# Attention and a gated MLP on one core: the low part of v's last tokens moves to GpSimd, the table is called early, and the written-out order is replaced

## The chip, the cores and the metric

The kernel runs on one core of a Trainium2 chip. Five instruction streams run side by side there: TensorE (matmuls; its weight loads are a row of their own in the profile, PEld), VectorE (DVE), ScalarE (ACT), GpSimd (POOL) and SyncE (SP), which issues the DMAs here. Each stream runs its instructions in the order in which they were written; semaphores make one wait for another. The metric is device time in microseconds, less is better.

## The reference

Causal attention over 4 batches, 12 heads, 448 tokens and 64 channels a head is followed by a gated MLP over all tokens of a batch, everything in float32:

```python
scores = scale * np.matmul(q, k.transpose(0, 1, 3, 2))
scores = np.where(mask, -1000000000.0, scores)
attn = np.exp(scores - np.max(scores, axis=-1, keepdims=True))
attn = attn / (np.sum(attn, axis=-1, keepdims=True) + 1e-09)
x = np.matmul(attn, v)              # heads side by side: (4, 448, 768)
h = x @ w_in                        # (4, 448, 1024), then gelu (tanh form)
u, v = h[..., :512], h[..., 512:]
v_n = (v - mu) / np.sqrt(var + 1e-06) * g_ln
v_s = np.einsum('ts,bsd->btd', w_sg, v_n) + b_sg[None, :, None]
out = x + (u * v_s) @ w_out
```

## The kernel before

Heads go in pairs: 24 pairs, six for each batch. For a pair, TensorE makes the scores (line 431, two groups of matmuls), DVE adds the mask and finds the maximum of each row (446), and ACT takes exponentials with the row sums (454, ten for a pair of five widths). The probabilities are then transposed: for the first eight pairs by TensorE (496), with the results copied out of PSUM by ACT or DVE (503, 501), for the others by DVE (484) and four DMAs. TensorE multiplies them with the values (522), DVE scales the result by the reciprocal row sums (549), and the product x is kept in a rounded high part and the low part that is left over (555 to 560).

The MLP of a batch has four kinds of matmul groups, all on line 577. Group v makes the half of h that is normed, for four blocks of tokens (128, 128, 128 and 64); group u makes the other half; group s multiplies the normed v with w_sg; group o multiplies with w_out. Precision is kept by splitting each operand into a high and a low part, each in the rounded format that TensorE reads fast, and adding three products. The weights are split when they arrive (366 to 374 for w_in and w_out, 350 to 353 for w_sg): ACT and DVE take the words apart, GpSimd rounds and subtracts.

For the first three token blocks of v, ACT writes the high part (630) and GpSimd subtracts it from the value (631). The last block has 64 tokens. Its high part goes to partitions 0 to 63 of the tile `vn3` (635) and its low part to partitions 64 to 127 of the same tile, so that one matmul takes both. Before the change, DVE makes that low part (636). The matmuls of group s that read `vn3` come last in each of its four groups.

Nothing of the order is left to a scheduler. Every step is recorded with its engine and an estimated duration (`od.add`, and `act`, `dve`, `pool_tt`, `pe`, `dma` over it), and a list of 1883 numbers, `ORDER`, says in which sequence the steps are written. The sequence on one engine is the sequence of that engine's steps in the list. PSUM has eight banks that all tiles there share: a new tile takes the bank that was given up first, and its first writer waits for the last reader of the old one. The estimated durations and the flag `port` were for the search that made the list; they don't reach the chip.

Before the first use of an exponential, ACT must load its table. Step 3 of the list, an exponential of one column into a spare tile, is meant to call for that load:

```python
    od.add("act", 0.2, lambda: nc.scalar.activation(out=pad[:, 0:1], in_=mhalf, func=AF.Exp), ["sm0"], ["table"])
```

Nothing depended on it, and in the old list it stands in the middle. Seven matmuls on a zeroed tile (339) are for warming TensorE up; their place is also the list's.

Of the kernel before, what the change touches and what calls it, by code (L numbers as in the profile page):

```python
# [12 lines left out]
AF = mybir.ActivationFunctionType  # L13
# [212 lines left out]
def attention_gated_mlp(ctx: ExitStack, tc: tile.TileContext, qk, vP, w_in, g_ln, w_sgT, b_sg, w_out, out):  # L226
# [100 lines left out]
    od.add("dve", 0.75, consts2, w=["P0", "sm0"])  # L327
    od.add("pool", 2.4, consts3, w=["P", "sm", ("wsg", "pad")])

    od.add("act", 0.2, lambda: nc.scalar.activation(out=pad[:, 0:1], in_=mhalf, func=AF.Exp), ["sm0"], ["table"])  # L330

    def warm():
        w = wz.t.bitcast(BF16)
# [432 lines left out]
```

## Time and profile before

| | us |
|---|---|
| median of 3 runs | 339.13 (338.38 to 340.37) |
| profiled execution | 337.29 |
| its span | 335.5 |
| busy in the span: TensorE, DVE, ACT, GpSimd | 324.1, 251.0, 208.5, 175.9 |
| mean granted clock of TensorE, as a share of full speed | 0.994 |

The span runs from the first to the last instruction of the program; the profiled execution has 1.8 us around it. Busy time of TensorE is the time in which some matmul was under way, so it also holds the small gaps between pipelined matmuls. An engine's share of the whole span is a mean over stages with different limits: ACT, for instance, is busy all the time early and little later.

### The profile page before, as it was taken

What the parts mean: (1) busy time and instruction counts of PE and PEld (TensorE: products, weight loads), DVE (VectorE), ACT (ScalarE), POOL (GpSimd) and SP (SyncE); (2) the same over time, 40 slices, a digit from 0 to 9 for tenths busy, and PEclk for the clock granted to TensorE, in tenths of its full rate; (3) what the DMA queues carried; (4) which work ended last, traced back from release to release, by engine and by line L of the source; (5) the groups of instructions that cost most, each with busy time, mean ns of one, the idle gap of its engine ahead of it and who ended that gap; (6) DMA issues with size and microseconds to landing.
All of it is one profiled execution on the core that took longest, in us unless ns stands there. A gap on an engine that the chain in (4) does not pass through costs nothing.

```text
span 335.5 us, 7568 instructions
## 1 busy us (share of the span) xinstructions
PE 324.1 (97%) x2590; PEld 266.3 (79%) x2591; DVE 251.0 (75%) x762; ACT 208.5 (62%) x674; POOL 175.9 (52%) x225
## 2 busy tenths in 40 slices
PE   5699999999999999999999999999999999999995
PEld 3467678768887987878888978878989987889994
DVE  4899898999999888967977597889788531644613
ACT  1999999999894637666784526486674302355210
POOL 4258766888986964020535942014256824132691
PEclk9899999999999999999999999999999999999999
DMA  7889968595583688638747858739437440010004
GB/s 227 312 247 307 277 218 267 177 288 160 130 265 103 178 215 235 197 98 226 217 127 214 229 150 204 195 95 243 101 104 206 91 159 3 0 55 2 18 36 164
DMA packets 30965, 56.55 MB, mean 169 GB/s; under 512 B 6096, under 2 KB 15056, under 8 KB 30928
## 3 DMA queue, kind: packets, MB, share of 16 engines
q1 hardware_dynamic: 30928, 56.08, 57.5%
q8 instruction: 20, 0.33, 0.4%
q14 instruction: 17, 0.14, 0.1%
HBM read 33.39 MB, written 5.90 MB: 117 GB/s over the span
## 4 chain that ended last, share of the span: by engine, by line
PE 93%; ACT 4%; DMA 1%; DVE 1%; issue 0%; ACTq 0%; DVEq 0%
PE m L577 65%; PE o L522 13%; PE s L431 11%; ACT P L454 3%; PE ty L496 2%; PE tx L496 2%; DMA qk<-in_qk_dram 1%; PE m L339 0%; ACT L454 0%; ACT vn L366 0%; ACT B L503 0%; DVE s L446 0%; DVE res L702 0%; DVE ngm L446 0%; ACTq L454 0%
## 5 line engine op out<-in xcount | busy, mean ns | idle before, releaser
L454 ACT ACTIVATE P<-s,ngm 128x320 f32<-128x320 f32 (+3 forms) x240 | 102.7, 460 | 28.1 <-DVE ngm L446 19.7
L446 DVE CUSTOM_DVE_ANT_0 s<-s,mask 64x64 f32<-64x64 f32 (+3 forms) x192 | 77.6, 435 | 7.5 <-PE s L431 5.8
L577 PE MATMUL m<-win,x 128*128 128x512 f32 (+1 forms) x264 | 65.9, 399 | 0.0
L577 PE MATMUL m<-g,wout 128*128 128x448 f32 x288 | 61.1, 367 | 0.0
L577 PE MATMUL m<-x,win 128*128 128x448 f32 x288 | 61.1, 367 | 0.0
L577 PEld LDWEIGHTS m<-x,win 128*128 128x128 f32 x288 | 53.9, 188 | 5.0
L577 PEld LDWEIGHTS m<-g,wout 128*128 128x128 f32 x288 | 53.9, 188 | 5.0
L577 PEld LDWEIGHTS m<-win,x 128*128 128x128 f32 (+1 forms) x264 | 47.4, 183 | 11.7
L454 ACT ACTIVATION_READ_ACCUMULATOR P<-s,ngm 128x1 f32 (+1 forms) x240 | 55.1, 233 | 0.0
L431 PE MATMUL s<-qk 64*64 64x64 f32 (+5 forms) x768 | 45.2, 371 | 5.0 <-DMA qk<-in_qk_dram 4.4
L431 PEld LDWEIGHTS s<-qk 64*64 64x64 f32 x768 | 30.7, 139 | 21.6 <-issue 8.5
L522 PE MATMUL o<-B,vraw 128*64 128x64 f32 (+4 forms) x672 | 45.0, 291 | 0.0
L522 PEld LDWEIGHTS o<-B,vraw 128*64 128x64 f32 x672 | 32.8, 137 | 12.7 <-issue 4.5
L484 DVE STREAM_TRANSPOSE P<-P 128x1024 f32<-128x1024 f32 x32 | 38.2, 1224 | 0.7 <-DMA B<-P 0.6
L577 PE MATMUL m<-wsg,vn 128*128 128x448 f32 x176 | 38.3, 369 | 0.0
L621 POOL TENSOR_TENSOR mv<-mv,mhalf 128x1 f32<-128x1 f32 (+1 forms) x16 | 10.0, 626 | 49.0 <-DVE mv L619 40.7
L577 PEld LDWEIGHTS m<-wsg,vn 128*128 128x128 f32 x176 | 32.6, 188 | 3.6 <-DVE vn L636 0.4
L558 POOL TENSOR_TENSOR x<-xt,x 128x448 fp32r<-128x448 f32 x24 | 27.5, 1148 | 14.5 <-ACT x L557 14.2
L702 DVE TENSOR_TENSOR res<-m,res 128x448 f32<-128x448 f32 (+1 forms) x25 | 14.8, 603 | 23.2 <-PE m L577 15.2
L586 DVE SCALAR_TENSOR_TENSOR tmp<-tmp,m 128x448 f32<-128x448 f32 (+1 forms) x28 | 17.9, 640 | 16.2 <-ACT tmp L585 16.0
L673 POOL TENSOR_TENSOR tmp<-tmp,g 128x448 f32<-128x448 f32 x16 | 18.3, 1152 | 18.8 <-DVE tmp L669 18.8
L585 ACT ACTIVATE tmp<-m 128x448 f32<-128x448 f32 (+1 forms) x28 | 15.5, 562 | 20.3 <-PE m L577 19.2
(76 smaller groups left out, 410.8 us busy)
## 6 DMA issues: line engine op xcount, KB each, us to landing
B<-P SPq DMA_DIRECT2D x64, 256.0 KB
qk<-in_qk_dram SPq DMA_DIRECT2D x24, 448.0 KB
vn<-in_w_in_dram SPq DMA_DIRECT2D x12, 512.0 KB
vraw<-in_vP_dram SPq DMA_DIRECT2D x24, 256.0 KB
rb<-rd SPq DMA_DIRECT2D x24, 224.0 KB
out_dram<-res SPq DMA_DIRECT2D x9, 448.0 KB
g<-in_w_out_dram SPq DMA_DIRECT2D x16, 192.0 KB
out_dram<-res SPq DMA_DIRECT2D x5, 224.0 KB
```

What stands on the lines that cost most here:

```text
L431: nc.tensor.matmul(out=s[z][bk].t[64 * h:64 * h + 64, col:col + n], lhsT=qk_.t[r, 0, q0:q0 + 64], rhs=qk_.t[r, 1, k0:k0 + n], start=True, ...
L446: nc.vector.tensor_tensor_reduce(out=o, in0=i, in1=mk, scale=-0.125, scalar=3e38, op0=ALU.add, op1=ALU.min, accum_out=ngm[ib[z]][c][0:m])
L454: act(n, lambda c=c, m=m, k0=k0, n=n, bk=bk, col=col, off=off, kc=kc, i=i, z=z: nc.scalar.activation(out=P[i][0:m, off:off + n], in_=s[z][ ...
L484: dve(PW, lambda z=z: nc.vector.transpose(A[ia][:, :, :, z, :].rearrange("p g t k -> p t g k"), P[ib[z]]), Pk[z] + [kp], Ak, 1.105)
L496: nc.tensor.transpose(out, P[ib[z]][:, col:col + 128], ident)
L522: nc.tensor.matmul(out=dst(o.t[r]), lhsT=vr.t[:, c, r], rhs=src(z), start=first and n == 0, stop=last and n == len(lst) - 1)
L558: pool_tt(S, lambda: nc.gpsimd.tensor_tensor(out=y.t[:, S + 64:], in0=x.t, in1=f(y.t)[:, 0:S], op=ALU.subtract), [x, y], [(y, 1)])
L577: nc.tensor.matmul(out=ps.t[0:l().shape[1], 0:n], lhsT=l(), rhs=rr(), start=(k == 0), stop=(k == len(mms) - 1))
L585: act(n, lambda: nc.scalar.activation(out=z(), in_=h(), func=AF.Square), [ps], [t])
L586: dve(n, lambda: nc.vector.scalar_tensor_tensor(out=z(), in0=z(), scalar=1.0 / GC, in1=h(), op0=ALU.add, op1=ALU.mult), [ps], [t])
L673: pool_tt(S, lambda z=z, u=u: nc.gpsimd.tensor_tensor(out=z(), in0=z(), in1=u.t, op=ALU.mult), [u], [t])
L702: dve(hi - lo, lambda rr=rr, ps=ps, z=z, lo=lo, hi=hi: nc.vector.tensor_tensor(out=rr.t[:, z, lo:hi], in0=ps.t[:, lo:hi], in1=rr.t[:, z, l ...
```

## The change

Three things change in the program, and with them the list.

1. The low part of v's last 64 tokens: DVE's subtraction goes. ACT writes the high part a second time, to partitions 64 to 127 of `vn3`, and copies the value to partitions 64 to 127 of its own tile; GpSimd then subtracts in place, with everything on those partitions. A batch has one DVE step less and two ACT steps and one GpSimd step more.
2. Every exponential of the attention depends on step 3, the call for the table.
3. The list has 1891 numbers, from a search in which DVE and GpSimd exclude each other where both need the SBUF port that they share. It differs from its beginning on. Step 3 stands early, for instance, GpSimd's two blocks of constants (steps 0 and 2) trade places, and so do two of DVE's memset blocks (1 and 4); some of w_out's loads and splits (steps 12 to 83 are those of w_in, later numbers those of w_out) come earlier and w_in's later.

Some estimates of durations and two `port` flags change too; they were for the search alone.

```diff
-    84, 85, 86, 1, 4, 0, 2, 89, 87, 90, 96, 88, 95, 98, 91, 92, 97, 99, 93, 94, 125, 126, 128, 127, 12, 18, 13, 103,
-    101, 116, 166, 332, 14, 129, 130, 20, 15, 102, 100, 134, 131, 135, 136, 19, 104, 138, 110, 111, 24, 344, 350, 356,
...
+    2, 4, 84, 85, 1, 0, 125, 86, 126, 127, 89, 87, 3, 90, 96, 88, 95, 98, 97, 91, 92, 99, 344, 345, 350, 93, 94, 101,
+    100, 128, 346, 129, 103, 108, 110, 104, 136, 102, 132, 133, 12, 18, 166, 109, 138, 111, 140, 13, 142, 20, 134,
...
-    od.add("act", 0.2, lambda: nc.scalar.activation(out=pad[:, 0:1], in_=mhalf, func=AF.Exp), ["sm0"], ["table"])
+    od.add("act", 1.35, lambda: nc.scalar.activation(out=pad[:, 0:1], in_=mhalf, func=AF.Exp), ["sm0"], ["table"])
...
-                    [s[z][bk], ("ngm", i, c), kp, ks] + ([("P", i, k - 1)] if k == 1 else [("P", i, 2)] if k == 4 else []),
+                    [s[z][bk], ("ngm", i, c), kp, ks, "table"] + ([("P", i, k - 1)] if k == 1 else [("P", i, 2)] if k == 4 else []),
...
-        od.add("dve", 0.42, inv, sk + [ks], [("rT", ip)])
+        od.add("dve", 0.573, inv, sk + [ks], [("rT", ip)])
...
-            tensor=rd[ip].tensor, offset=rd[ip].offset, ap=[[512, 8], [0, 16], [1, S]])), [("rd", ip)], [rb], 320e3, dur=0.56)
+            tensor=rd[ip].tensor, offset=rd[ip].offset, ap=[[512, 8], [0, 16], [1, S]])), [("rd", ip)], [rb], 360e3, dur=0.56)
...
-                t, z = gelu2(hs, m, DH)
+                t, z = gelu2(hs, m, DH, port=True)
...
-                out=z(), in_=z(), func=AF.Identity, scale=mv.t[0:m, 1:2], bias=mv.t[0:m, 2:3]), [mv], [t], True)
+                out=z(), in_=z(), func=AF.Identity, scale=mv.t[0:m, 1:2], bias=mv.t[0:m, 2:3]), [mv], [t], True, 2)
...
-                dve(DH, lambda y=y, z=z: nc.vector.tensor_tensor(out=y.t[64:128], in0=z(), in1=f(y.t)[0:64],
-                                                                 op=ALU.subtract), [t, y], [(y, 1)])
+                act(DH, lambda y=y, z=z: nc.scalar.activation(out=y.t[64:128], in_=z(), func=AF.Copy), [t], [(y, 1)], True)
+                act(DH, lambda t=t, z=z: nc.scalar.activation(out=t.t[64:128], in_=z(), func=AF.Copy), [], [t], True)
+                pool_tt(DH, lambda y=y, t=t: nc.gpsimd.tensor_tensor(out=y.t[64:128], in0=t.t[64:128],
+                                                                     in1=f(y.t)[64:128], op=ALU.subtract), [t], [(y, 1)])
```

## Rows read from the trace of the kernel before

**Rows 1.** The chain of waits in order of time: start us, us, what.

```profile
3.92 1.88 PE s L431 x8
...
8.37 1.40 ACT P L454 x5
...
13.46 0.56 ACT vn L366
...
18.85 0.61 ACT P L454 x2
...
20.00 0.66 PE ty L496 x4
...
276.38 55.46 PE m L577 x263
...
331.87 0.62 DVE res L702
```

**Rows 2.** Busy time by stretches: stretch, length, busy of each engine, granted clock, DMA.

```profile
20.00:40.00 20.00, 19.95 (x226) 13.94 (x228) 18.91 (x79) 20.00 (x79) 14.24 (x17) 1.00 0.91 271
60.00:80.00 20.00, 20.00 (x186) 14.54 (x185) 19.65 (x68) 19.32 (x67) 16.39 (x22) 1.00 0.78 238
80.00:100.00 20.00, 20.00 (x121) 17.36 (x120) 18.96 (x63) 17.45 (x54) 18.25 (x24) 1.00 0.59 168
100.00:120.00 20.00, 20.00 (x170) 16.90 (x172) 17.73 (x44) 11.17 (x37) 16.64 (x21) 1.00 0.55 147
```

**Rows 3.** Timeline of DVE and ACT in the front: start, us, engine, instruction, idle before.

```profile
5.94 0.23 DVE L446 CUSTOM_DVE_ANT_0 s<-s,mask 64x64 f32<-64x64 f32 x1 [3.88 <-PE s L431]
...
7.07 1.28 ACT L454 ACT_TABLE_LOAD   x1 [7.07 <-DVE ngm L446]
...
21.18 0.40 ACT L454 ACTIVATE P<-s,ngm 64x64 f32<-64x64 f32 x1
...
21.47 0.69 ACT L503 ACTIVATE B<-tx 128x512 f32<-128x512 f32 x1
21.95 0.62 ACT L454 ACTIVATE P<-s,ngm 128x320 f32<-128x320 f32 x1
...
22.45 0.79 ACT L366 ACTIVATE vn<-vn 128x512 f32<-128x512 f32 x1
```

**Rows 4.** Timeline of TensorE, 20 to 24 us.

```profile
20.97 1.67 PE L339 MATMUL m<-tmp 128*128 128x512 bf16 x6
22.58 1.64 PE L431 MATMUL s<-qk 64*64 64x448 f32 x26
```

**Rows 5.** Waits of the weight loads, 22 to 332 us: total, times, longest.

```profile
PEld s L431 <- ACT B L503: 0.8, 2, 0.4
...
PEld m L577 <- DVE vn L636: 0.4, 2, 0.2
```

**Rows 6.** Groups by form: busy us, mean ns of one, idle before.

```profile
L631 POOL TENSOR_TENSOR vn<-tmp,vn 128x512 fp32r<-128x512 f32 x12 | 15.9, 1331 | 18.5 <-ACT vn L630 18.4
...
L635 ACT ACTIVATE vn<-tmp 64x512 fp32r<-64x512 f32 x4 | 2.5, 630 | 0.1
```

**Rows 7.** The view of line 636: durations are min/median/max in ns.

```profile
L636 DVE TENSOR_TENSOR vn<-tmp,vn x4: 685/685/2120, 97.8 to 308.4; 64x512 fp32r<-64x512 f32 x4
```

**Rows 8.** Timeline around the low part's subtraction, batches 0 and 2.

```profile
98.51 0.30 PEld L577 LDWEIGHTS m<-wsg,vn 128*128 128x128 f32 x2 [0.18 <-DVE vn L636]
...
243.78 2.27 POOL L689 TENSOR_TENSOR res<-x 128x448 f32<-128x448 f32 x2
...
244.48 2.12 DVE L636 TENSOR_TENSOR vn<-tmp,vn 64x512 fp32r<-64x512 f32 x1 [1.02 <-ACT vn L635]
...
246.65 0.30 PEld L577 LDWEIGHTS m<-wsg,vn 128*128 128x128 f32 x2 [0.25 <-DVE vn L636]
```

**Rows 9.** Busy time and granted clock of TensorE, 14 to 18 us.

```profile
14.00:18.00 4.00, 3.64 (x28) 0.57 0.51 157
```

More of the change, by code (lines that the diff above doesn't have):

```diff
@@ L579, in group, with gelu2 @@
             pe(per * len(mms[a:a + cut]), go, rd, [ps])
-    def gelu2(ps, m, n, dst=None):
+    def gelu2(ps, m, n, dst=None, port=False):
         t = buf(three, "tmp", [128, 512])
@@ L586, in gelu2 @@
         dve(n, lambda: nc.vector.scalar_tensor_tensor(out=z(), in0=z(), scalar=1.0 / GC, in1=h(), op0=ALU.add,
-                                                      op1=ALU.mult), [ps], [t])
+                                                      op1=ALU.mult), [ps], [t], port=port)
         act(n, lambda: nc.scalar.activation(out=z(), in_=z(), func=AF.Tanh, scale=GS * GC), [], [t], True)
@@ L590, in gelu2 @@
         dve(n, lambda: nc.vector.scalar_tensor_tensor(out=z() if dst is None else d.t, in0=z(), scalar=1.0, in1=h(),
-                                                      op0=ALU.add, op1=ALU.mult), [ps, t], [d])
+                                                      op0=ALU.add, op1=ALU.mult), [ps, t], [d], port=port)
         return t, z
@@ L622, in mlp @@
                 out=mv.t[0:m, 1:2], in0=mv.t[0:m, 1:2], in1=mhalf[0:m], op=ALU.pow), ["sm0"], [mv])
-            od.add("dve", 0.07, lambda mv=mv, m=m: nc.vector.tensor_scalar(
+            od.add("dve", 0.125, lambda mv=mv, m=m: nc.vector.tensor_scalar(
                 out=mv.t[0:m, 2:3], in0=mv.t[0:m, 0:1], scalar1=mv.t[0:m, 1:2], scalar2=-1.0, op0=ALU.mult, op1=ALU.mult),
```

177 rows, old and new, of the table ORDER are left out of this document.

## Prediction

> **What bounds the kernel now.** The profiled execution took 337.29 us, 335.5 of them its span; the runs shown have the median 339.13 (338.38 to 340.37). I make the sum against the profiled one and carry the difference over to the median.
>
> I read the chain of waits in order of time first. The reader is to see three stretches in it. From 3.92 to 8.37 it runs through the scores of the first pair, their maxima on DVE and the load of the activation table on ACT. From 8.37 to 20.0 it stays on ACT, but for fractions of a microsecond. From 20.0 to 331.8 it is TensorE alone, and then comes one DVE addition and the store [rows 1, 3]. So whatever TensorE does first at full density comes sooner or later, and the end moves with it, unless another engine then makes TensorE wait.
>
> The busy time by stretches says who could. Between 20 and 40 us ACT is busy for 20.00 of 20 us and DVE for 18.91; between 60 and 80 us DVE for 19.65 and ACT for 19.32; between 80 and 100 us GpSimd has its peak, 18.25. After 100 us ACT falls to 11.17 [rows 2]. So up to some 80 us three engines run nearly full beside TensorE, and later TensorE alone decides.
>
> Third, the waits of TensorE's weight loads from 22 us on: those on ACT are fractions of a microsecond (on ACT's evictions 0.8 in two), and those on the low part of v's last tokens, DVE's instruction that the change takes away, are 0.4 in two [rows 5]. TensorE runs just behind ACT, and there is little to win after 22 us.
>
> **The change, part by part.**
>
> *The table.* The first ACT instruction of the old list is an exponential. The load of the table stands before it: ACT sits idle for 7.07 us, then loads for 1.28, and the first exponential starts at 8.37 [rows 3, 1]. The new list puts the small exponential that calls for the table first on ACT and makes every other exponential depend on it. It needs only DVE's memsets, and DVE is done with those 3.88 us before its first maximum at 5.94 [rows 3]. So the load is over by about 3.6 us, in time in which ACT has nothing to do; that idle time is its cover, and without it the 1.30 (8.37 less 7.07) would come back. This takes 1.30 us off the chain.
>
> The Trainium skill, in ScalarE: Activation LUTs, What ACT_TABLE_LOAD costs, gives 1283 ns for the load and about 1380 more for a drain. The load agrees with the row; the drain isn't there, since the next ACT instruction starts 0.02 us after the load, and by the page's 2.66 us the sum would be 1.36 us lower.
>
> *The order in the front.* The scores of pair 3 are the first work of TensorE's dense stretch whose place both lists share: they start at 22.58, after warm-up matmuls that end there [rows 4]. In the new list their second bank waits for the same eviction as before, the one of pair 1 that starts at 21.47 [rows 3] and ends near 22.2. Both lists have 31 ACT steps up to it. The old has two exponentials of pair 2 (448 and 64 wide) and a third split of w_in that the new has not; the new has one exponential of 320 and one split of w_out instead, beside the small one for the table. From start to start a 448-wide one, a split, a 64-wide and a 320-wide one cost 0.61 (the piece at 18.85) and 0.56 (at 13.46) [rows 1], 0.29 (21.18 to 21.47) and 0.50 (21.95 to 22.45) [rows 3]; I price the narrower w_out split at the same 0.56. That is 0.61 + 0.29 - 0.50 = 0.40 less, and 1.30 from the table: 1.7. So the eviction ends near 20.5, and the scores, whose start no longer trails the warm-up matmuls (the new list mixes these among the transposes), start there: 2.1 us earlier than 22.58.
>
> *What ACT lets TensorE keep.* The rest of ACT's work isn't gone, only listed later. For each matmul that waits for an ACT step I added the ACT work listed ahead of that step and the TensorE work listed behind the matmul, both at the durations of the trace. The largest sum bounds the end. In the old list it is 43.1 + 275.5 us (100 ACT steps ahead of the first scores of pair 8, 2103 matmuls behind); in the new one 56.7 + 261.6 us (134 and 1996, at the second scores of pair 9). A step of ACT costs 0.3 to 0.6 as above, a matmul of the late groups 55.46/263 = 0.21 [rows 1]. The sums differ by 0.3, the start of ACT by 1.30: the end may come 1.6 us earlier by this bound, 0.5 less than the front gives. I take 1.6.
>
> DVE's bound I can't fix so well. Its first maximum waits for scores [rows 3] that don't move, so it gains nothing at the start, and it is 91 to 98% busy up to 100 us [rows 2]. If it is the engine that TensorE trails, the gain is between 0 and 1.6.
>
> *The low part of v's last 64 tokens.* Out go four subtractions on DVE, 685 ns in the median and 2120 once [rows 7]; in come eight copies on ACT like the one that was there (630 ns) and four subtractions on GpSimd, for which the nearest row is the one over 128 partitions, 1331 ns [rows 6]. All lie behind 80 us, where ACT has room, so the engines' time costs nothing; what it would cost without that room is 5.0 us of ACT. The path from a batch's last v group to the first matmul that reads its low part grows by two copies and by 1331 against 685: 1.26 + 0.65 = 1.9 us. In batches 0 and 2, at 98.5 and 246.65, TensorE's weights waited for just this subtraction [rows 5, 8], so there is no slack in the old list; the new one puts 21.0 instead of 19.2 us of TensorE work between the two in batch 0, and 19.9 instead of 16.4 in batch 2. That leaves -0.1 and +1.6. In batches 1 and 3 nothing waited; the lists leave the same work in batch 1 and 0.6 more in batch 3. So I take nothing for it, with 0 to 1.9 us a batch as its bounds.
>
> *The port.* The trace shows what the shorthand means: DVE's subtraction with both inputs in SBUF starts at 244.48 beside GpSimd's additions (243.78 to 246.05) and takes 2.12 us; TensorE's weights wait for it until 246.65 [rows 8]. An order that avoids such meetings can win on TensorE's path the 0.4 of [rows 5] at most; I take 0.2. The other estimates that the diff changes (the Identity's, the transfer's, the reciprocal's) are numbers for the planner and alter no instruction; they act by the list alone.
>
> *The end.* Both lists finish with one 448-wide addition and its store, as in the row at 331.87 [rows 1]: nothing.
>
> Sum: -1.6 - 0.2 = -1.8 us. The profiled execution would take 335.5 (a span of 333.7) and the median 339.13 - 1.8 = 337.3.
>
> **The rivals.**
>
> *DVE hands it back.* TensorE starts its dense stretch 2.1 us earlier and then trails DVE, whose start hasn't moved. For it: DVE's 19.65 of 20 us; against it: TensorE's weights wait longer for ACT's evictions than for DVE's subtraction [rows 2, 5]. Half the gain is left, -0.9: 338.2.
>
> *It does not do what it says.* TensorE loses all of it by 80 us: 339.1. Against it: ACT is gap-free from 8.37 to 20.0, and the 1.30 is a plain removal [rows 1].
>
> *The subtraction comes late, and the kernel is slower.* On GpSimd it waits behind the splits of w_out in batch 0, where that engine is 18.25 of 20 us busy [rows 2], and the list's 1.8 us doesn't cover it. Batches 0 and 3 at 1.9 us each make +3.8, less 1.8: +2.0, 341.1. It decides from 3.5 us of such waits on. The Trainium skill speaks for this one: GPSIMD Engine Reference, Engine selection, would have elementwise work on VectorE, GpSimd being about twice as slow with two inputs. Here the rows make it 1331 to 685, which agrees [rows 6, 7].
>
> *The clock.* Between 14 and 18 us TensorE's granted clock averaged 0.57 [rows 9], so it was at the lower of its two levels (1.2 GHz) for most of that time, after a stretch with single transposes and waits. The chain was on ACT then, so it cost nothing. If such a stretch comes when TensorE is already dense, 4 x 0.43 = 1.7 us of work is lost: 339.0.
>
> **How the numbers follow.** The bound for telling a difference is 0.5%, 1.7 us: 337.4. The forecast, 337.3, lies just beyond it. Chances: the forecast or better 0.45, DVE hands it back 0.28, no effect 0.08, late subtraction 0.13, clock 0.06. So faster 0.45, same 0.28 + 0.08 + 0.06 = 0.42, slower 0.13. The lower end takes the whole front and all collisions, 2.1 + 0.4, and a run's scatter of 0.6: 336.0. The upper end leaves out most of the late subtraction: 340.2. The forecast's own range is 336.4 to 338.0.
>
> **What would show it.** The table's load before 4 us and the first exponential at 7.1; the scores of pair 3 near 20.5; DVE without its four subtractions, GpSimd with four more subtractions of about 1.3 us; no wait of TensorE for the low part over 0.3 us. I am wrong if TensorE waits for DVE or ACT again between 25 and 80 us (the gain is handed back), or for GpSimd's subtraction.

## The result: 1.1% slower, and the profile after

| | before | after |
|---|---|---|
| median, us (runs) | 338.94 (4) | 342.85 (4) |
| ratio, 95% interval | | 1.0109 (1.0078 to 1.014) |
| profiled execution, us (span) | 337.29 (335.5) | 342.85 (341.0) |

One of the changed kernel's four runs took 348.29 us at a lower granted clock and is left out of the ratio. The forecast was 337.3 us, in a range of 336.0 to 340.2: wrong in sign, by 5.5 us. By the medians the change costs 3.9 us; the two traces differ by more, 5.5 us in the span, since the traced execution of before is 1.65 us under its median. The front did what the prediction says. On the timeline of ACT and TensorE (start, us, engine, instruction) the table is loaded at once, the first exponential starts at 7.09 instead of 8.37 [rows 3], and the dense scores start at 20.11 instead of 22.58 [rows 4]:

```profile
0.73 1.28 ACT L331 ACT_TABLE_LOAD   x1 [0.73 <-PEq L758]
...
7.09 0.64 ACT L455 ACTIVATE P<-s,ngm 128x448 f32<-128x448 f32 x1 [4.79 <-DVE ngm L447]
...
20.11 1.88 PE L432 MATMUL s<-qk 64*64 64x448 f32 x32
```

Then TensorE gives it all back and more. The busy times by stretches (columns as in [rows 2]):

```profile
20.00:40.00 20.00, 18.91 (x229) 13.11 (x228) 19.01 (x77) 19.63 (x84) 11.91 (x15) 1.00 0.79 254
40.00:60.00 20.00, 19.04 (x189) 14.48 (x190) 19.61 (x66) 18.79 (x67) 15.21 (x19) 1.00 0.82 243
60.00:80.00 20.00, 17.16 (x153) 11.74 (x152) 19.79 (x56) 15.72 (x56) 15.78 (x22) 1.00 0.61 173
80.00:100.00 20.00, 20.00 (x137) 16.83 (x137) 18.91 (x59) 16.14 (x50) 14.71 (x16) 1.00 0.78 231
100.00:120.00 20.00, 18.94 (x148) 16.04 (x145) 19.46 (x46) 12.11 (x30) 18.93 (x28) 1.00 0.53 143
```

TensorE was full in the stretches of [rows 2] before. Now it has gaps from 20 us on, most from 60 to 80, where DVE is at 19.79 of 20 and ACT only at 15.72. The granted clock is 1.00 throughout, so the clock is not it. The chain of waits by engine, first of the kernel before:

```profile
PE 93%; ACT 4%; DMA 1%; DVE 1%; issue 0%; ACTq 0%; DVEq 0%
```

and of the changed one, with pieces of that chain (start, us, what) between 55 us and the end:

```profile
PE 73%; DVE 13%; ACT 6%; DMA 3%; issue 2%; POOL 1%; SPq 1%; DVEq 0%; ACTq 0%
...
55.24 1.30 DVE g L369
...
56.56 1.21 DVE g L371
...
63.40 1.08 DVE vn L371
...
86.90 6.78 DMA g<-in_w_out_dram
93.71 0.93 DVE g L369
95.65 1.13 DVE g L369
...
105.33 1.37 DVE g L371
106.69 1.06 DVE tmp L587 x2
107.75 1.16 DVE P L485
...
281.45 55.89 PE m L578 x266
...
337.37 0.62 DVE res L705
```

DVE's share goes from 1 to 13%. Its longest pieces are its two operations on the weights (the shift, line 369, and the shift with OR, 371; 368 and 370 before), for w_out (`g`) and w_in (`vn`): 17.6 of the 41.0 us that DVE has on the chain between 20 and 112 us. From 80.29 to 93.71 us the chain leaves DVE for GpSimd's work on the weights, the issue of transfers and a load of w_out (6.78 us); DVE stood still for that load for 0.6 us. The same operations by form, 20 to 110 us (busy us, mean ns), before:

```profile
L370 DVE SCALAR_TENSOR_TENSOR vn<-vn 128x512 int32<-128x512 int32 x10 | 6.9, 691 | 0.3 <-ACT vn L366 0.2
L370 DVE SCALAR_TENSOR_TENSOR g<-g 128x192 int32<-128x192 int32 x16 | 6.2, 405 | 0.0
L368 DVE TENSOR_SCALAR g<-g 128x192 int32<-128x192 int32 x16 | 5.0, 333 | 0.0
L368 DVE TENSOR_SCALAR vn<-vn 128x512 int32<-128x512 int32 x9 | 3.9, 428 | 0.0
```

and after:

```profile
L371 DVE SCALAR_TENSOR_TENSOR g<-g 128x192 int32<-128x192 int32 x16 | 9.4, 595 | 0.1
L369 DVE TENSOR_SCALAR g<-g 128x192 int32<-128x192 int32 x15 | 8.8, 590 | 0.6 <-DMA g<-in_w_out_dram 0.6
L371 DVE SCALAR_TENSOR_TENSOR vn<-vn 128x512 int32<-128x512 int32 x10 | 7.4, 742 | 0.0
L369 DVE TENSOR_SCALAR vn<-vn 128x512 int32<-128x512 int32 x10 | 6.2, 618 | 0.0
```

It is 51 operations in both, 22.0 us before and 31.8 after: DVE doesn't do more of them, they take longer. Why shows on the timeline of DVE and GpSimd after, 55 to 63 us:

```profile
55.08 1.32 POOL L375 TENSOR_TENSOR win<-vn,win 128x512 fp32r<-128x512 f32 x1
55.16 1.36 DVE L369 TENSOR_SCALAR g<-g 128x192 int32<-128x192 int32 x1
56.37 1.18 POOL L354 TENSOR_TENSOR wsg<-tmp,wsg 128x448 fp32r<-128x448 f32 x1
56.56 1.21 DVE L371 SCALAR_TENSOR_TENSOR g<-g 128x192 int32<-128x192 int32 x1
...
61.40 1.26 POOL L559 TENSOR_TENSOR x<-xt,x 128x448 fp32r<-128x448 f32 x1
...
61.98 0.96 DVE L369 TENSOR_SCALAR vn<-vn 128x512 int32<-128x512 int32 x1
```

A shift that starts beside a GpSimd operation ends just after that one ends: GpSimd is done at 56.40, the shift at 56.52; then 57.55 and 57.77; then 62.66 and 62.94. I call this a meeting. The Trainium skill, in SBUF — State Buffer, SBUF: two separate sides, says of a GpSimd instruction and a DVE instruction that has two inputs in SBUF or runs in a mode with two ports: the one that starts first gets the shared port pair for its whole instruction and the other fully blocks. The trace agrees in these three pairs; whether the shift, which has one input, runs in such a mode no run here shows.

To see where the time goes I count TensorE's own work in the order of its list (each step at its usual duration in the trace of before) and give, where N us of it are done, the time minus N. A number that grows is time lost. The columns e1 to e17 are experiments below.

```
N us    before  after   e1     e9     e12    e15    e16    e17
 10     12.62   10.13  11.51  10.11  10.14  11.31  10.04  11.44
 20     13.38   10.68  12.92  10.73  10.44  12.06  10.33  12.37
 35     14.28   11.98  14.21  11.64  11.50  13.94  11.91  13.23
 45     14.83   13.20  14.96  13.62  13.00  14.86  12.59  13.78
 55     15.31   18.08  15.81  15.18  13.97  15.32  13.73  14.24
 85     16.21   20.37  16.75  16.90  15.02  16.32  14.88  15.11
110     16.46   21.22  16.98  17.59  15.79  16.52  15.30  15.31
```

Each column is one execution, so differences of 1 to 2 us between columns can be scatter: the trace of before is 1.65 us under its median, that of e12 the fastest of its twelve (337.93 us, median 338.82). After is 2.7 us ahead at N = 20 and 4.8 behind at N = 110 (131 us into the run); from 109.47 us on, the chain after is TensorE's, as it was before. Between N = 10 and 110 TensorE loses 3.8 us before and 11.1 after, a difference of 7.3; against e1, the old list with the table early, it is 5.6. By the minima of each form (244, 315, 415 and 674 ns in the trace of before) the 51 operations need 19.4 us in the old list and 19.6 in the new one; 2.6 and 12.2 us are on top. In the new list 24 operations are more than 0.15 us over their minimum, 11.9 us in all; every one of them starts while a GpSimd instruction is running, and 23 of them end 0.12 to 0.29 us after one ends. In the old list it is 6 operations, with 2.3 us. So what is on top is nearly all meetings.

### The profile page after: what moved, and what is told of

It is laid out like the page before. It is cut to its first block, busy times and chain, and to the rows that moved or that the text cites. A ratio compares the mean times of both kernels' runs of the same rounds, so it can differ in the third digit from the quotient of the medians.

```text
span 341.0 us, 7550 instructions
## 1 busy us (share of the span) xinstructions
PE 324.8 (95%) x2591; PEld 265.1 (78%) x2591; DVE 255.2 (75%) x758; ACT 213.5 (63%) x682; POOL 180.1 (53%) x229
## 4 chain that ended last, share of the span: by engine, by line
PE 73%; DVE 13%; ACT 6%; DMA 3%; issue 2%; POOL 1%; SPq 1%; DVEq 0%; ACTq 0%
PE m L578 54%; PE o L523 9%; PE s L432 8%; ACT P L455 5%; DVE s L447 3%; DVE g L371 2%; DMA g<-in_w_out_dram 2%; DVE g L369 2%; DVE P L485 1%; DMA qk<-in_qk_dram 1%; PE ty L497 1%; DVE ngm L447 1%; DVE vn L371 1%; ACT B L504 1%; PE tx L497 1%
## 5 line engine op out<-in xcount | busy, mean ns | idle before, releaser
L455 ACT ACTIVATE P<-s,ngm 64x64 f32<-64x64 f32 (+3 forms) x240 | 100.5, 433 | 31.4 <-DVE ngm L447 26.2
L432 PE MATMUL s<-qk 64*64 64x128 f32 (+5 forms) x768 | 44.8, 369 | 5.4 <-DMA qk<-in_qk_dram 3.9
L455 ACT ACTIVATION_READ_ACCUMULATOR P<-s,ngm 128x1 f32 (+1 forms) x240 | 49.6, 207 | 0.0
L432 PEld LDWEIGHTS s<-qk 64*64 64x64 f32 x768 | 29.9, 138 | 22.3 <-issue 8.9
L559 POOL TENSOR_TENSOR x<-xt,x 128x448 fp32r<-128x448 f32 x24 | 28.3, 1186 | 31.5 <-ACT x L558 31.4
L632 POOL TENSOR_TENSOR vn<-tmp,vn 128x512 fp32r<-128x512 f32 x12 | 15.5, 1295 | 28.7 <-ACT vn L631 28.7
L692 POOL TENSOR_TENSOR res<-x 128x448 f32<-128x448 f32 x24 | 27.6, 1163 | 2.7 <-DMA out_dram<-res 2.5
L589 ACT ACTIVATE tmp<-tmp 128x448 f32<-128x448 f32 (+2 forms) x32 | 19.2, 603 | 15.4 <-DVE tmp L587 15.3
L587 DVE SCALAR_TENSOR_TENSOR tmp<-tmp,m 128x448 f32<-128x448 f32 (+1 forms) x28 | 17.6, 638 | 13.8 <-ACT tmp L586 13.8
```

The costliest lines, as they stand in the source:

```text
L432: nc.tensor.matmul(out=s[z][bk].t[64 * h:64 * h + 64, col:col + n], lhsT=qk_.t[r, 0, q0:q0 + 64], rhs=qk_.t[r, 1, k0:k0 + n], start=True, ...
L455: act(n, lambda c=c, m=m, k0=k0, n=n, bk=bk, col=col, off=off, kc=kc, i=i, z=z: nc.scalar.activation(out=P[i][0:m, off:off + n], in_=s[z][ ...
L559: pool_tt(S, lambda: nc.gpsimd.tensor_tensor(out=y.t[:, S + 64:], in0=x.t, in1=f(y.t)[:, 0:S], op=ALU.subtract), [x, y], [(y, 1)])
L587: dve(n, lambda: nc.vector.scalar_tensor_tensor(out=z(), in0=z(), scalar=1.0 / GC, in1=h(), op0=ALU.add, op1=ALU.mult), [ps], [t], port=port)
L589: act(n, lambda: nc.scalar.activation(out=z(), in_=z(), func=AF.Tanh, scale=GS * GC), [], [t], True)
L632: pool_tt(DH, lambda y=y, z=z: nc.gpsimd.tensor_tensor(out=y.t[:, 1, :], in0=z(), in1=f(y.t)[:, 0, :], op=ALU.subtract), [t, y], [(y, 1)])
```

## The experiments

The theories, numbered as in the expectations: 1, the new list makes DVE meet GpSimd at the port, and DVE sets TensorE's pace between 35 and 110 us; 2, the moved low part costs the time; 3, a lead at the front is eaten later in any list; 4, the new list puts more DVE work ahead of the first batch's tokens; 5, it converts w_in too late. "Excess" is the time of DVE's steps over the usual one of their kind: the 8.8 us in e5's expectation is a coarser count of what is 13 to 14.5 by the lower quartile of a kind. Ratios are to the kernel before, timed beside each, with 95% intervals.

### Parts alone

**e1, the table alone**, in the old list:

```diff
-    84, 85, 86, 1, 4, 0, 2, 89, 87, 90,
+    84, 85, 86, 1, 4, 3, 0, 2, 89, 87, 90,
...
-    1207, 1208, 3, 1211, 1213,
+    1207, 1208, 1211, 1213,
```

> The program and the list of before, with step 3 alone (the load of the table of exponentials) moved from near the end of the front to the start of ScalarE's queue. By the prediction's term for the table, 1.3 us come off ScalarE's first exponential and, if the front is held by it all the way to TensorE, 1.3 us off the time: 337.6 us. If the start of TensorE's gapless stretch hangs on the other steps of the old list's front (the loads and VectorE's conversions), the exponential moves and the time stays within 0.5 us of before: 338.4 to 339.4.

337.53 us, 0.9976 (0.9956 to 0.9997). The first exponential starts at 7.17, and TensorE is 1.1 us ahead at N = 10, but 0.1 at N = 35. In DVE's waits between 8 and 62 us stands where it stops (total, times, longest):

```profile
DVE xt L549 <- DMA rb<-rd: 2.4, 2, 1.3
```

DVE multiplies by the reciprocal row sums, which go out to DRAM and back, and came no earlier. So 1.3 us of table is 0.8 us of time, give or take 0.7.

**e8, the table, with two of those multiplications later** (steps 162 and 326, pairs 1 and 5; their followers on GpSimd move along):

```diff
-    188, 161, 120, 121, 162, 198, 239, 122, 123, 124, 163, 165, 164, 585, 192, 193, 196, 197, 249, 251, 623, 252, 225,
+    188, 161, 120, 121, 198, 239, 122, 123, 124, 585, 192, 193, 196, 197, 249, 251, 623, 252, 162, 163, 164, 165, 225,
```

> The first experiment (table early, old list) with two of VectorE's multiplications by the reciprocal row sums (line 549, of pairs 1 and 5) moved a few steps later in the list, because VectorE stood still before them, 1.13 and 1.25 us, until the reciprocals came back from DRAM. If that standing still is what ate the lead of 1.1 us, 336 to 337.2; if the reciprocals' round trip is only met again one step later (GpSimd, the first matmuls of the gated part), 337.2 to 338.2, as the first experiment.

337.46 us, 0.9953 (0.9931 to 0.9974), and between 8 and 100 us no wait of DVE for the row sums is left in its list of waits. It beats before and after. That it beats e1 isn't shown: the intervals overlap.

**e2, the low part alone**, in the old list, in the place of DVE's subtraction (step 511; later numbers shift by two):

```diff
-    509, 510, 520, 530, 838, 842, 511, 538,
+    509, 510, 522, 532, 840, 844, 511, 512, 513, 540,
```

> The list of before with only the low part changed: two copies by ScalarE and one subtraction by GpSimd stand where VectorE's subtraction stood, four times; the table's load stays where it was and the exponentials do not depend on it. Theory 1 (the loss is the new list's, in VectorE's meetings with GpSimd at the port between 35 and 110 us): within 0.7 us of before, 338.3 to 339.7, and TensorE waits for GpSimd's subtraction by less than 0.3 us a batch. Theory 2 (the loss is the moved low part): 1 us a batch at GpSimd and ScalarE, 342 to 343.

346.09 us, 1.0231 (1.0192 to 1.027). TensorE's waits:

```profile
PE m L578 <- POOL vn L639: 4.6, 3, 3.4
```

That is 4.6 of the 7.9 us; the rest is not traced. On the timeline of ACT one sees why in batch 0: two tanhs (line 589) and two exponentials (455, at 99.49 and 100.12 us, left out below) stand ahead of the two copies (637, 638).

```profile
98.55 1.03 ACT L589 ACTIVATE tmp<-tmp 128x448 f32<-128x448 f32 x2
...
100.53 0.63 ACT L637 ACTIVATE vn<-tmp 64x512 fp32r<-64x512 f32 x1
101.07 0.61 ACT L638 ACTIVATE tmp<-tmp 64x512 f32<-64x512 f32 x1
```

**e7, the low part well placed**: as e2, the copies directly behind the rounding copy (510):

```diff
-    509, 510, 522, 532, 840, 844, 511, 512, 513, 540,
+    509, 510, 511, 512, 513, 522, 532, 840, 844, 540,
```

> The list of before with the new low part as in the second experiment, but with ScalarE's two copies directly behind its rounding copy in each batch, so that no other work of ScalarE or GpSimd stands between. If the second experiment's 8 us come from where the copies stood (four operations of ScalarE ahead of them in the first batch, about 1.9 us): 341 to 343.5, the rest being the longer chain itself, 0.63 + 0.63 + 1.28 us with its waits in place of VectorE's 0.69 us, where the old list has no slack. If the chain itself has slack, 338 to 339.5. If the copies' place is not the cause, 345 to 347.

341.07 us, 1.0059 (1.0037 to 1.0081); the wait above shrinks to 2.2 us. So in the old list the longer path costs about 2 us where its copies are well placed, and four times that in e2's place.

**e3, the new list with the old low part**:

```diff
-    842, 511, 512, 436, 407, 396, 513, 397,
+    840, 436, 407, 396, 511, 397,
```

> The new list, with the low part back on VectorE: its one subtraction stands where GpSimd's stood, and the two copies by ScalarE are gone. Theory 1 (the list, meetings at the port): VectorE still loses 7 to 9 us more than its usual durations between 32 and 107 us, and the time stays at 342 to 343.5. Theory 2 (the low part): the front's gain of 3 us shows and nothing is given back, 336 to 338.

344.48 us, 1.0184 (1.0143 to 1.0225): no faster than the change. This alone doesn't settle theory 2, since e3's trace has a loss that the changed kernel has not: one transfer of row sums stands on its chain for 11.26 us (from 44.28 us on), and TensorE then waits 3.1 us for q and k. In the changed kernel, where DVE waits only 0.4 us for row sums between 20 and 110 us, no wait of TensorE for the low part is listed, and GpSimd's subtraction has its expected size (min/median/max ns):

```profile
L639 POOL TENSOR_TENSOR vn<-tmp,vn x4: 1271/1294/1297, 105.2 to 312.4; 64x512 fp32r<-64x512 f32 x4
```

So the new list hides the low part, and theory 2 falls by the changed kernel's own trace: the loss is the list's.

### Three edits of the list that went wrong

**e4, the front of the new list, then the old order** (the first 209 numbers of the new list, the others as in the old one):

```diff
-    266, 264, 262, 290, 294, 291, 388, 298, 292, 296,
+    266, 264, 262, 290, 294, 291, 36, 28, 29, 33, 34, 38,
```

> The changed program, with the new list up to TensorE's second scores of pair 5 (about 33 us) and the remaining steps in the old list's order. Theory 1 (the loss comes from the list between 35 and 110 us): the front's gain of about 3 us stays in part, since the old order loses under 2 us to the port there: 336 to 338. Theory 3 (whoever is early in the front is held later by the total of VectorE's work before 100 us, in whatever order): the lead of 3 us is eaten by 110 us, 338.5 to 341. Theory 2 (the low part): 342 or more.

351.04 us, 1.0373 (1.0336 to 1.0411). The chain:

```profile
29.96 5.53 DMA vn<-in_w_in_dram
```

The new front loads w_out early and w_in late; the old order behind it then wants pieces of w_in that were not loaded yet. It tells that the two lists can't be cut and joined, and nothing on theory 3.

**e6, w_out's steps no earlier than in the old list; e11, w_in's no later.** A piece of each list, without and with the edit:

```diff
-    298, 292, 296, 299, 352, 305, 268, 307, 295,
+    246, 374, 376, 364, 352, 345, 346, 347, 443,
...
-    629, 636, 382, 320, 38, 440, 357, 638, 627,
+    224, 222, 347, 289, 38, 37, 42, 35, 48,
```

> The changed kernel with its new list, except that the steps of w_out's 16 pieces come no earlier against TensorE's steps than in the old list; 16 of VectorE's 32 operations on w_out move later by it. Theory 4 (VectorE's w_out work ahead of the first batch's tokens holds them back): the tokens' first gate on VectorE comes at 68 us or before instead of 73.3, and the time falls to 338.5 to 341. Theory 1 (port): the pieces meet GpSimd's wherever they stand, VectorE's excess stays near 8 us and the time within 1 us of 342.8.

> The changed kernel with its new list, except that the steps of w_in's 12 pieces (load, conversion, split) come no later against TensorE's steps than in the old list; 22 of VectorE's 24 operations on w_in move earlier by it. Theory 5: TensorE has its gated work early again (16 us of it done by 70 us instead of 10.5) and the loss of 7 us between 35 and 105 us shrinks to under 3: 336 to 339.5. Theory 1 (port): VectorE's meetings with GpSimd remain in number, the excess stays over 9 us, 341 to 344. A way for it to go wrong under both: the front's scores and exponentials come later by the work put ahead of them, and the lead at TensorE's 20th us of work (2.7 us) goes.

353.72 us (1.0434, 1.0407 to 1.046) and 368.67 us (1.0874, 1.0835 to 1.0912). In both, loads come onto the chain (in e6 a piece of w_in for 7.3 us at 53 us); in e11 ACT and DVE stand 8.4 and 8.1 us at w_in's conversions, waiting for loads, with all their other work queued behind. They fail by what the edits broke and decide nothing between theories 4 and 5.

### GpSimd's side of the meetings

**e5, GpSimd's operations on w_out cut to 16 of 192 columns**, the rest filled with a constant:

```diff
+        w = 16 if key[0] == "wout" else n
-        od.add("pool", ..., lambda: nc.gpsimd.tensor_copy(dst(0), f(lo())), ...)
+        od.add("pool", ..., lambda: nc.gpsimd.tensor_copy(dst(0)[:, 0:w], f(lo())[:, 0:w]), ...)
...
+        nc.vector.memset(f(wout)[:, :, 1, :], 0.0)
```

> The changed kernel with GpSimd's two operations on each piece of w_out (the rounding copy and the subtraction) cut from 192 columns to 16, so that GpSimd holds the port for some 14 us less before 110 us; the other columns of w_out's two parts are only filled with a constant at the start, so the output product is not the reference's. Nothing else of VectorE's work or order changes. Theory 1 (meetings with GpSimd at the port): VectorE's excess over its usual durations falls from 8.8 us to under 5, TensorE's lead of 3 us over before is kept in part, 338 to 340.5. Theory 4 (simply more VectorE work listed ahead of the first batch's tokens, 59.6 us against 53.0): the excess may fall, but 342 to 343.5 stays.

346.44 us, 1.0213 (1.0188 to 1.0239). My fill came between DVE's first maxima and cost the front 3.1 us; from N = 10 to 110 TensorE loses 11.2 us, as in the changed kernel, and the excess stays (14.8 against 14.5). So these were not DVE's main partners.

**e9, GpSimd's subtractions on w_in and w_sg cut to 16 columns**, which are the partners in the timeline above; **e14, the same in the kernel before**:

```diff
-        pool_tt(n, lambda: nc.gpsimd.tensor_tensor(out=dst(1), in0=f(lo()), in1=f(dst(0)), op=ALU.subtract),
+        w = 16 if key[0] == "win" else n
+        pool_tt(n, lambda: nc.gpsimd.tensor_tensor(out=dst(1)[:, 0:w], in0=f(lo())[:, 0:w], in1=f(dst(0))[:, 0:w],
...
+        nc.vector.memset(f(win)[:, 0:2, 1, :], 0.0)
+        nc.scalar.activation(out=win[:, 2:KC, 1, :], in_=mhalf.unsqueeze(2).to_broadcast([128, KC - 2, DF]), func=AF.Copy,
+                             scale=0.0)
```

> The changed kernel with GpSimd's subtraction on each piece of w_in (512 columns) and of the gate's weights (448) cut to 16 columns; the low parts' other columns are filled with a constant by VectorE and ScalarE in the first 6 us, where both wait, so the output is not the reference's. These subtractions are the partners in 8 of VectorE's 16 longest meetings between 20 and 110 us of the changed kernel (5.1 us of 10.2). Theory 1 (port): VectorE's excess falls from 13.3 us by about 5, and TensorE's loss between its 10th and 110th us of work (11.1 us in the changed kernel, 3.8 in the one before) falls by 3 to 5, total 338 to 340.5. Theory 5 (the new list has w_in's pieces converted too late for TensorE: the last of the v half at 52.8 us against 41.1): the loss stays at 9 to 12 us, total 341 to 343.5, since the places of the steps are unchanged.

> The control to the ninth: the same cut of GpSimd's subtractions on w_in and the gate's weights to 16 columns, in the kernel before (ScalarE's constant fill stands behind VectorE's in the first 7 us). VectorE's excess over its usual durations is 5.0 us there between 20 and 110 us against 14.5 in the changed kernel. Theory 1 (the new list's meetings): under 0.7 us to be had, 337.8 to 339.2. If less GpSimd work helps any kernel here, 2 to 3 us come off as in the ninth.

e9 takes 339.66 us, 1.0030 (1.0006 to 1.0053): with the same front the loss falls from 11.1 to 7.5 us and the excess from 14.5 to 9.5, as theory 1 has it. But e14 takes 336.03, 0.9916 (0.9891 to 0.9942). Part of that is the table: ACT's constant fill loads it, and no second load stands ahead of the exponentials:

```profile
0.73 1.28 ACT L325 ACT_TABLE_LOAD   x1 [0.73 <-PEq L761]
2.02 3.62 ACT L325 ACTIVATE win<-mhalf 128x4096 fp32r<-128x4096 f32 x1
7.20 0.63 ACT L460 ACTIVATE P<-s,ngm 128x448 f32<-128x448 f32 x1 [1.56 <-DVE ngm L452]
```

Against e1 the cut is worth 0.60% in the old list, and 0.79% in the new one. So shorter GpSimd work helps either list nearly alike, and e9 doesn't show that the meetings are the new list's loss.

### VectorE's side

**e10, e12, e16**: in the changed kernel, the OR on w_out cut to 16 columns; on w_in too; both operations on both, with GpSimd reading ACT's half of the pair instead. **e13** is e12's cut in the kernel before, **e15** and **e17** are the cuts of e12 and e16 in e1. The lines of e16:

```diff
-        dve(n, lambda: nc.vector.tensor_scalar(out=lo(), in0=lo(), scalar1=29, ...
+        dve(n, lambda: nc.vector.tensor_scalar(out=lo()[:, 0:16], in0=lo()[:, 0:16], scalar1=29, ...
-        dve(n, lambda: nc.vector.scalar_tensor_tensor(out=lo(), in0=hi(), scalar=3, in1=lo(), ...
+        dve(n, lambda: nc.vector.scalar_tensor_tensor(out=lo()[:, 0:16], in0=hi()[:, 0:16], scalar=3, in1=lo()[:, 0:16], ...
```

> The changed kernel with VectorE's second operation (shift and OR) on each of w_out's 16 pieces cut from 192 columns to 16, so w_out is wrong. It takes 16 times some 0.28 us off VectorE and the meetings of these operations, 2.9 us more: 7 us. Theory 4 (VectorE's amount of work ahead of the first batch's tokens is what TensorE waits for): 4 to 6 us come back, 336.5 to 339. Theory 5 (the places of w_in's steps, which also wait for loads and buffers): under 3 us come back, 340 to 342.5. If VectorE is not the bound at all, 342 to 343.5.

> The changed kernel with VectorE's second operation (shift and OR) on every piece of w_in and w_out cut to 16 columns, so both matrices are wrong. It takes some 10 us of work off VectorE before 110 us, and the meetings of these operations with GpSimd. If all of the loss between TensorE's 10th and 110th us of work (11.1 us in the changed kernel, 3.8 in the one before) comes from VectorE being the bound there (its work and its meetings), the loss falls to 4 to 6 us: 335.5 to 338. If part of it lies in loads and buffers that the new list places late, it stays at 8 to 10: 339.5 to 342.

> The control to the twelfth: the same cut of VectorE's second operation to 16 columns, in the kernel before. There TensorE is gapless from 20 us, so with VectorE not the bound it gives under 0.7 us: 337.8 to 339.2. If less work of VectorE helps any kernel of this kind, 2 us or more come off here too, and the twelfth says nothing of the change.

> The control to the twelfth with a lead to lose: the first experiment (old list, table early, 337.53 us) with VectorE's second operation on w_in and w_out cut to 16 columns. If VectorE also eats the lead of the old list, the lead of about 1.1 us at TensorE's 10th us of work is kept to the end and over 1 us comes off the first experiment: 335.5 to 336.7. If something else eats it (the round trip of the row sums through DRAM, the loads of w_in that wait for their buffers), 337 to 338.

> The changed kernel with both of VectorE's operations on every piece of w_in and w_out cut to 16 columns; GpSimd then reads ScalarE's half of the pair instead, at the same width and stride, so only the values of both matrices are wrong. Between 20 and 110 us these operations (51 of them) take 31.8 us in the changed kernel and 22.0 in the one before. If VectorE, its work and its meetings, is all that sets the new list behind the old, the kernel is no slower than the seventeenth: both at 334 to 336.5, since its front is ahead. If about half lies elsewhere (the twelfth against the fifteenth left 2.2 us), it stays 2 us or more behind the seventeenth: 337 to 339.

> The control to the sixteenth: the same cut of VectorE's two operations to 16 columns, in the first experiment (old list, table early, 337.53 us). The fifteenth, with one of the two operations cut, took 337.05. If VectorE has a small share in this list, 335.5 to 337; if it has none any more, 336.7 to 337.3.

| DVE's work on the weights | new list | old list, table early | new over old |
|---|---|---|---|
| whole | after: 1.0109 | e1: 0.9976 | 1.33% |
| OR on w_out cut | e10: 1.0061 (1.0033 to 1.0089) | | |
| OR cut | e12: 1.0005 (0.9986 to 1.0023) | e15: 0.9941 (0.9917 to 0.9965) | 0.64% |
| both cut | e16: 0.9944 (0.9922 to 0.9965) | e17: 0.9924 (0.9900 to 0.9948) | 0.20% |

The last column is a quotient of two ratios and uncertain by some 0.3 to 0.4%. e10, for some 4.5 us less of DVE's work, gives back 0.48%, 1.6 us, less than theory 4 asks (4 to 6 us); its 340.95 us lies in the range that its expectation gives to theory 5. e12's 338.82 lies between its two ranges. e16 ends 0.6 us behind e17, where its expectation asked for no slower if DVE is all, and for 2 us or more if half lies elsewhere. e13, the control without the early table, is at 0.9980 (0.9960 to 1.0001): DVE's work matters little to the kernel before. What sets the new list behind the old goes away with DVE's work on the weights: 1.33, 0.64, 0.20%, the last within its uncertainty. In the table of TensorE's losses e16 keeps most of the lead, 5.3 us lost between N = 10 and 110 against 11.1. A part stays there: with the work whole the new list loses 5.6 us more than the old one with the table early (e1), with both cut 1.4 us more (e17). So loads and buffers (theory 5) aren't needed for most of it; that they have a part in the last 1.4 us isn't excluded.

Does DVE lose by its own work, or by meetings? In e16 the operations have 16 columns and next to no work, but (min/median/max ns, 20 to 110 us):

```profile
L371 DVE SCALAR_TENSOR_TENSOR g<-g x16: 157/174/1189, 25.0 to 99.0; 128x16 int32<-128x16 int32 x16
L371 DVE SCALAR_TENSOR_TENSOR vn<-vn x10: 127/337/1068, 25.6 to 86.1; 128x16 int32<-128x16 int32 x10
```

An operation of some 0.16 us lasts up to 1.19. That is waiting, and so are, by the count of starts and ends above, nearly all of the 9.8 us which the whole operations take longer after than before. How many of TensorE's 7.3 us they alone cost, and how many fall to theory 4, stays open: e9 took only meetings away, but its control gained too.

## Why the prediction was wrong, step by step

- *The table*: right in place and size at ACT, 1.28 us for 1.30; the load itself was over at 2.01 us, not near 3.6, for it waited for no memset. Alone it is worth 0.8 us (e1), since the row sums' way through DRAM holds DVE next.
- *The order in the front*: right. Expected near 20.5, seen at 20.11.
- *What ACT lets TensorE keep*: this failed, in its last paragraph. The sum over ACT's steps was no longer the bound: by it the second scores of pair 9 could start 56.7 us after the first exponential, at 63.8 us; they start at 68.9, and ACT had stood idle for 3.2 us in one piece before. "DVE's bound I can't fix so well" left DVE between 0 and 1.6 us of gain, from its busy share alone, and 1.6 was taken into the sum. DVE had to do 51 operations on weights beside GpSimd in a new order, and its rows were never summed by list. Where the sum has a gain of 1.6 us, the span grew by 5.5 (the medians by 3.9).
- *The port*: this failed in sign. One meeting on TensorE's path was priced, as a gain of 0.2 with 0.4 at most; no bound was given for new meetings of DVE's other operations, though the row of 2.12 us for 0.69 [rows 7, 8] was there to price them: eight of that size make 11 us on DVE. The traces show 12.2 us on top of the minima against 2.6.
- *The low part*: nothing for it, right in the new list, where no wait of TensorE for it is listed. In the old list the bound of 1.9 us a batch holds where the copies are well placed (e7's four batches cost 2.0 us in all), and not in e2, where one batch waits 3.4.
- *The end*: right; the last addition and store are the same.
- The rivals: *DVE hands it back* had the right engine, but gave back half of the gain at most. Its own price allowed no loss, since I let the old list's DVE time stand for the new one's. *It does not do what it says* had the place right, for the lead is gone by 80 us (N = 55), but stopped at nothing. *The subtraction comes late* is what e2 shows, there for ACT's copies, and not the change. *The clock*: granted 1.00 in all stretches above.

The line "I am wrong if TensorE waits for DVE or ACT again between 25 and 80 us" is what happened, though TensorE's own list of waits shows little of it: it shows on the chain.

## What to carry to other kernels

A lead won at the front is kept only if the engine that is next in line has room: before one prices a new order, each engine's steps are to be summed along it, and for VectorE with its meetings. Where VectorE is 90% busy beside GpSimd, as here, each of its operations that can meet a GpSimd operation has two durations, alone and until the other ends, and the second belongs in the range. That a search kept the two engines apart at the port is a claim about its estimates: here the meetings grew, from 2.3 to 11.9 us on the weights.

## What the runs showed of the hardware

A tiny operation meets as long as a big one. Halving a column of gains, 128x4, takes DVE 149 ns in the old list; in the new one it stands beside GpSimd's subtractions on w_in, which are done at 52.79 us, and ends at 52.82:

```profile
L396 DVE TENSOR_SCALAR gcol<-gcol 128x4 f32<-128x4 f32 x1 | 1.3, 1260 | 0.0
```

And the table of exponentials needs no exponential to call for it: in e14 a Copy at 2.02 us was preceded by the one load there is, and the first exponential followed at 7.20 without another.
